# Second product of a mixture of experts: twenty products on blocks of four by three in place of seven on two by two

## The chip, the cores and the metric

The kernel runs on one core of one Trainium2 chip. The metric is device time in microseconds from launch to end, the median of several runs. All data is float32.

## The reference, cut to what matters

An attention block with sketched keys and queries gives `attn_out`; it becomes `x`, 4352 tokens of 128 values. Then comes a mixture of 8 experts, in which every token goes through every expert and is weighted by a matrix `P` that is balanced over rows and columns in turn:

```python
N, D, E, F = (4352, 128, 8, 1024)
logits = x @ w_gate
P = np.exp(logits - logits.max())
for _ in range(8):
    P /= P.sum(1, keepdims=True) + 1e-09
    P /= P.sum(0, keepdims=True) + 1e-09
    P *= N / E
for e in range(E):
    h = np.maximum(x @ w1[e], 0.0)      # first product, F = 1024 wide
    out += P[:, e:e + 1] * (h @ w2[e])  # second product
```

## The kernel before

Everything lies with features on the partitions and tokens along the free dimension. `xT` is x turned; `w1[e]` is 128 x 1024, that is 8 row blocks f of 128; `w2[e]` has 8 blocks f of 128 rows, each with two halves of 64 outputs. Every matmul of the two products has 64 output columns of weights (`tile_position=(0, H2 * s)`), so that two of them, one for the lower (s = 0) and one for the upper half (s = 1), can run beside each other on TensorE.

The unit of work is an **item**: one expert on a pair of token tiles, 2 x 480 tokens (2 x 256 for the first 512). An item has four **quads**, each of two row blocks f by two tiles. In a quad, `first(k, c)` makes the first product of one row block and one tile (L686, two matmuls into a bank `a`), and ScalarE applies the relu into `h` (L690). `combine` lets VectorE form four sums of these (L696, L698, L699, tile `t`). `seven` then lists seven products (L735) that stand for eight: a 2 x 2 by 2 x 2 block product with seven multiplications. Some of their weights are blocks of `w2`, others are sums and differences of blocks, tile `ws`, which `load_w` lets GpSimd form once per expert (L183 to L186) and then keeps in DRAM (`stored`) for the later groups. The seven products add up in four PSUM banks `s0` to `s3` (`mps`), over all row blocks and all experts of a **group**; `part` adds the four banks up into the two output tiles when a group ends, one operation at a time (`soon`, `later`), and stores them.

The groups: five plain ones with expert 0 (one for each pair of tiles) and one with expert 1, whose results are kept (`kept`) since the weights P aren't known yet, and then five weighted ones with the other experts, whose source is `xe`, x times the weight of the expert, formed by GpSimd (L531, L533) from a row of `pT` that a DMA spreads over the partitions (`pb`). Kept results are weighted by `weigh_kept` at the second expert of the group. Plain groups fill TensorE while the attention and the routing run: `fill(n)` takes n steps from the generator `steps()`, each step being one `first`, one of VectorE's sums and two of the second products, of two quads before (`LAG = 2`).

Order: the part with attention and routing has a hand-written order on VectorE and TensorE (`tc.manual_schedule`); the rest, and all of GpSimd's and SyncE's queues, are ordered by a planner. Pool `wpool` holds weights for two experts, `aps` four banks for first products, `hpool` three quads of `h` and `t`.

Of the kernel before, what the change touches and what calls it, by code (L numbers as in the profile page):

```python
# [10 lines left out]
F32 = mybir.dt.float32  # L11
# [39 lines left out]
def kernel(  # L51
# [12 lines left out]
    nc = tc.nc  # L64
# [19 lines left out]
    hpool = ctx.enter_context(tc.tile_pool(name="hpool", bufs=3))  # L84
# [4 lines left out]
    keep = ctx.enter_context(tc.tile_pool(name="keep", bufs=1))  # L89
    early = ExitStack()  # L90
# [36 lines left out]
    lgT = big.tile([P, SA, 32], F32, name="lgT")  # L127
    lgp = big.tile([P, SA, 32], F32, name="lgp")
# [15 lines left out]
    loaded = {}  # L144
# [26 lines left out]
    def load_w(e):  # L171
# [3 lines left out]
        nc.sync.dma_start(out=w2, in_=moe_w2[e].rearrange("(fo fi) d -> fi fo d", fi=P))  # L175

        ws = wpool.tile([P, 4, FO // 2, H2], F32, tag="ws", name="ws")
        if e in stored:
            nc.sync.dma_start(out=ws, in_=stored[e])
            return w1, w2, ws  # L180
# [6 lines left out]
        if e:  # L187
            stored[e] = dram.tile([P, 4, FO // 2, H2], F32, name=f"ws{e}")
            nc.sync.dma_start(out=stored[e], in_=ws)
        return w1, w2, ws  # L190

    stored = {}
# [239 lines left out]
    def routing():  # L432
# [45 lines left out]
        for b in (1, 2, 0, 3):  # L478
            nc.sync.dma_start(out=pT[:, b * S:(b + 1) * S],
                                                  in_=lgT[32 * b:32 * b + E].rearrange("p a s -> p (a s)"))  # L480
# [4 lines left out]
    sizes = [256] * 2 + [480] * 8  # L485
    starts = [sum(sizes[:i]) for i in range(len(sizes))]
    assert sum(sizes) == N
    NP = len(sizes) // 2
    PLAIN = NP
    NMAX = max(sizes)  # L490

    def pair(i):
        return starts[2 * i], sizes[2 * i]

    plain = [(i, 0) for i in range(NP)] + [(1, 1)]
    groups = [(i, [e], False) for i, e in plain]
    groups += [(i, list(range(2 if i == 1 else 1, E)), True) for i in (2, 1, *range(3, NP), 0)]
    PLAIN = len(plain)  # L500
    items = [(g, e) for g, (_, es, _) in enumerate(groups) for e in es]
    loaded_w, sources, sums, kept, parts, done = {}, {}, {}, {}, {}, {}
    soon, later = [], []

    def prepare_w(j):
        if j == 0:
            loaded_w[j] = first_w
        elif items[j - 1][1] == items[j][1]:
            loaded_w[j] = loaded_w[j - 1]
        else:  # L510
            loaded_w[j] = load_w(items[j][1])

    def weights_of(e, i):
        lo, n = pair(i)
        pb = pools[0].tile([P, 2 * NMAX], F32, tag="pb", name="pb")[:, 0:2 * n]
        nc.sync.dma_start(out=pb, in_=pT[e:e + 1, lo:lo + 2 * n].to_broadcast([P, 2 * n]))
        return pb

    def prepare_x(j):
        g, e = items[j]  # L520
        i, es, weighted = groups[g]
        lo, n = pair(i)
        if not weighted:
            sources[j] = xT[:, lo:lo + 2 * n]
            return
        pb = weights_of(e, i)
        xe = pools[0].tile([P, 2 * NMAX], F32, tag="xe", name="xe")[:, 0:2 * n]
        if j == PLAIN:
            for t in range(2):
                sl = slice(t * n, (t + 1) * n)  # L530
                nc.gpsimd.tensor_tensor(xe[:, sl], xT[:, lo:lo + 2 * n][:, sl], pb[:, sl], op=Alu.mult)  # L531
        else:
            nc.gpsimd.tensor_tensor(xe, xT[:, lo:lo + 2 * n], pb, op=Alu.mult)  # L533
        sources[j] = xe

    def weigh_kept(i):

        n = pair(i)[1]
        es = [e for p, e in plain if p == i]
        for e in es:  # L540
            pb = weights_of(e, i)
            for t in range(2):
                y = kept[i, e][t]
                nc.gpsimd.tensor_tensor(y, y, pb[:, t * n:(t + 1) * n], op=Alu.mult)  # L544
        for t in range(2):
            for e in es[1:]:
                nc.gpsimd.tensor_tensor(kept[i, es[0]][t], kept[i, es[0]][t], kept[i, e][t], op=Alu.add)

    def part(g, k):

        i, es, weighted = groups[g]
        lo, n = pair(i)
        end = g == len(groups) - 1
        lower, upper = slice(0, H2), slice(H2, P)
        s = sums[g][k]

        def tile_(tag, pool=keep, bufs=1, width=NMAX):
            return pool.tile([P, width], F32, tag=tag, name=tag, bufs=bufs)[:, 0:n]

        def at_leisure(do):  # L560

            soon.append(lambda: later.append(do))
# [4 lines left out]
        def add_now(out, a, b):  # L567
            if end:
                nc.vector.tensor_tensor(out, a, b, op=Alu.add)
            else:  # L570
                soon.append(lambda: nc.vector.tensor_tensor(out, a, b, op=Alu.add))  # L571

        def put(t):
            y = (y1, y2)[t]
            b0, nb = (lo + t * n) // 32, n // 32
            yt = pools[0].tile([P, NMAX // 32, 32], F32, tag="yt", name="yt")[:, 0:nb, :]
            nc.vector.transpose(out=yt.rearrange("p b d -> p (b d)"), in_=y)
            store(yt, b0, b0 + nb, ends[t] if end else (nc.sync,))

        own = parts.setdefault(g, {})  # L580
        if end:
            if not own:
                own.update(y=[tile_(f"y{t}", pools[0], 2) for t in range(2)], z=tile_("z"), w=tile_("w"),
                           x=tile_("m"), f=tile_("f"), r=tile_("r"))
            (y1, y2), z, w, x, f, r = (own[a] for a in "yzwxfr")
            k1, k2 = kept[i, 0]
            if k == 3:
                nc.scalar.copy(w[lower], k2[lower])
                nc.scalar.copy(r[upper], s[lower])
                add_now(w[upper], s[upper], r[upper])  # L590
                add_now(x[upper], w[upper], k1[upper])
                add_now(w[upper], w[upper], k2[upper])
            elif k == 0:
                nc.scalar.copy(z[lower], s[upper])
                nc.vector.tensor_copy(z[upper], s[lower])
                add_now(z, s, z)
                add_now(x[upper], x[upper], z[upper])
                add_now(x[lower], s[lower], k1[lower])
                add_now(z, z, w)
            elif k == 2:  # L600
                nc.scalar.copy(f[lower], s[upper])
                nc.scalar.copy(f[upper], s[upper])
                add_now(z[lower], s[lower], z[lower])
                add_now(y2, z, f)
                put(1)
            else:
                add_now(y1, s, x)
                put(0)
            return
        if not own:  # L610
            if weighted:
                own["y"] = [tile_(f"y{t}", pools[0], 2) for t in range(2)]
                own["k"] = kept[i, es[0] if (i, es[0]) in kept else 0]
            else:
                own["y"] = kept[i, es[0]] = [tile_(f"y{i}{es[0]}{t}", keep, 1, n) for t in range(2)]
        y1, y2 = own["y"]
        if k == 0:
            z = own["z"] = tile_("z")
# [4 lines left out]
        elif k == 1:  # L623
            m = own["m"] = tile_("m")
            if weighted:
                add_now(m, s, own["k"][0])
            else:
                nc.scalar.copy(m, s)
            add_now(y1[lower], own["p1"][lower], m[lower])
        elif k == 2:  # L630
            w, f = own["w"], own["f"] = tile_("w"), tile_("f")
# [3 lines left out]
            if weighted:  # L635
                add(f, f, own["k"][1])
        else:
            r = tile_("r")
# [5 lines left out]
        if all(own.get(x) for x in (0, 2, 3)) and "v" not in own:  # L644
# [4 lines left out]
            if weighted:  # L649
                at_leisure(lambda: put(1))  # L650
        if all(own.get(x) for x in range(4)):
            add(y1[upper], z[upper], m[upper])
            if weighted:
                at_leisure(lambda: put(0))
# [15 lines left out]
    quads = [(j, q) for j in range(len(items)) for q in range(FO // 2)]  # L670
    LAG = 2
    hs = {}

    def first(k, c):

        j, q = quads[k]
        n = pair(groups[items[j][0]][0])[1]
        if c == 0:
            hs[k] = (hpool.tile([P, 4, NMAX], F32, tag="h", name="h")[:, :, 0:n],
                     hpool.tile([P, 4, NMAX], F32, tag="t", name="t")[:, :, 0:n])  # L680
        f, t = 2 * q + c // 2, c % 2
        ph = bank()[:, 0:n]
        order = (0, 1) if k % 2 == 0 else (1, 0)
        for s in order:
            sl = slice(H2 * s, H2 * (s + 1))
            nc.tensor.matmul(ph[sl], loaded_w[j][0][:, P * f + H2 * s:P * f + H2 * (s + 1)],  # L686
                             sources[j][:, t * n:(t + 1) * n], start=True, stop=True,
                             tile_position=(0, H2 * s))
        h, ts = hs[k]
        nc.scalar.activation(out=h[:, c], in_=ph, func=Act.Relu)  # L690

    def combine(k):

        h, ts = hs[k]

        nc.vector.tensor_tensor(ts[:, 0:2], h[:, 1::2], h[:, 0:2], op=Alu.subtract)  # L696
        yield
# [190 lines left out]
```

## Time and profile before

| | |
|---|---|
| median of 4 runs | 957.4 us (955.93 to 957.52) |
| the profiled execution, its own time | 956.35 us |
| its span, first to last instruction | 954.5 us |
| granted clock of TensorE | 0.997 |
| TensorE busy | 939.8 us (98%) |
| VectorE busy | 562.1 us (59%) |
| ScalarE busy | 393.8 us (41%) |
| GpSimd busy | 122.4 us (13%) |
| moved by DMA | 82.34 MB, 86 GB/s over the span |

The durations below come from the one profiled execution. In its lines, PE is TensorE, PEld its weight loads, DVE VectorE, ACT ScalarE, POOL GpSimd and SP SyncE; `out<-in` are tiles by their names, `L735` is a line of the kernel. A line of the timeline has the start in us from the start of the span, the duration, the engine and the instruction; `x4` merges four records that touch. A TensorE record ends later than its successor on the same half starts, since matmuls are pipelined: what one costs is the distance of starts.

### The profile page before, as it was taken

The page shows a single profiled execution, that of the slowest core. Times are in us where ns is not written, and L with a number is a line of the kernel's source. Part 1 is how long each engine was busy: PE and PEld are TensorE (multiplying, and loading weights), DVE is VectorE, ACT ScalarE, POOL GpSimd, SP SyncE. Part 2 cuts the span into 40 slices and gives each one's busy share as a digit, 9 for nine tenths or more (in the row PEclk, how much of TensorE's full clock was granted, in tenths as well). Part 3 has the DMA queues.
Part 4 walks back from the last instruction along what each step waited for, and adds up shares of the span by engine and source line. Part 5 has one row for each costly group of instructions (what it writes and reads, how often), then busy time and mean ns, then how long its engine had stood idle before and what let it go on. Part 6 is the DMA issues. An engine that isn't in the chain of part 4 may idle for free.

```text
span 954.5 us, 13484 instructions
## 1 busy us (share of the span) xinstructions
PE 939.8 (98%) x5506; PEld 453.2 (47%) x5506; DVE 562.1 (59%) x763; ACT 393.8 (41%) x754; POOL 122.4 (13%) x105
## 2 busy tenths in 40 slices
PE   8999999999999999999999999999999999999996
PEld 6553535456666666433333333333333333346664
DVE  7787679885555546744445644444564444457555
ACT  2444345553333335333335333333443333345443
POOL 1000000142222213200001000000200000011100
PEclk9999999999999999999999999999999999999998
DMA  6600000221222232622223422222242222236430
GB/s 191 183 23 1 1 1 1 93 84 65 87 88 87 88 109 64 172 85 84 82 87 101 107 86 86 87 88 84 88 119 83 86 77 76 76 93 169 146 111 12
DMA packets 75405, 82.34 MB, mean 86 GB/s; under 512 B 22416, under 2 KB 60304, under 8 KB 75344
## 3 DMA queue, kind: packets, MB, share of 16 engines
q1 hardware_dynamic: 74320, 81.29, 27.4%
q8 instruction: 43, 0.70, 0.3%
q10 hardware_dynamic: 960, 0.13, 0.1%
q14 instruction: 18, 0.15, 0.0%
q0 software_dynamic: 64, 0.07, 0.0%
HBM read 75.44 MB, written 6.04 MB: 85 GB/s over the span
## 4 chain that ended last, share of the span: by engine, by line
PE 94%; DVE 4%; DMA 1%; issue 0%; ACT 0%; DVEq 0%; POOL 0%; POOLq 0%
PE a L686 48%; PE s L735 42%; PE a L317 1%; PE a L339 1%; PE a L286 1%; DMA ws<-ws 0%; PE a L255 0%; DVE kp L271 0%; DVE t L699 0%; DMA raw<-in_S_dram 0%; DVE qa L329 0%; DVE kT L242 0%; DVE rd L356 0%; DVE qT L237 0%; DVE t L696 0%
## 5 line engine op out<-in xcount | busy, mean ns | idle before, releaser
L686 PE MATMUL a<-xe,w 128*64 128x480 f32 (+1 forms) x2176 | 637.0, 528 | 0.0
L690 ACT ACTIVATE h<-a 128x480 f32<-128x480 f32 (+1 forms) x640 | 341.4, 534 | 515.1 <-PE a L686 509.4
L696 DVE TENSOR_TENSOR t<-h 128x960 f32<-128x960 f32 (+1 forms) x160 | 216.0, 1350 | 346.3 <-ACT h L690 346.2
L735 PE MATMUL s<-t,ws 128*64 128x480 f32 (+1 forms) x960 | 419.0, 529 | 0.0
L686 PEld LDWEIGHTS a<-xe,w 128*64 128x64 f32 x2176 | 241.8, 137 | 210.7 <-issue 160.0
L735 PE MATMUL s<-h,w 128*64 128x480 f32 (+1 forms) x640 | 286.1, 529 | 1.0 <-DVE y L571 1.0
L735 PEld LDWEIGHTS s<-t,ws 128*64 128x64 f32 x960 | 130.7, 137 | 126.5 <-issue 108.1
L735 PE MATMUL s<-t,w 128*64 128x480 f32 (+1 forms) x320 | 143.0, 529 | 0.2
L735 PE MATMUL s<-h,ws 128*64 128x480 f32 (+1 forms) x320 | 143.0, 529 | 0.0
L533 POOL TENSOR_TENSOR xe<-xT,pb 128x960 f32<-128x960 f32 (+1 forms) x33 | 67.6, 2049 | 537.5 <-PE a L686 447.1
L686 PE MATMUL a<-xT,w 128*64 128x480 f32 (+1 forms) x384 | 113.2, 540 | 1.1 <-DVE xT L358 0.9
L699 DVE TENSOR_TENSOR t<-h,t 128x480 f32<-128x480 f32 (+1 forms) x160 | 105.5, 659 | 5.4
L698 DVE TENSOR_TENSOR t<-h,t 128x480 f32<-128x480 f32 (+1 forms) x160 | 103.7, 648 | 5.1
L735 PEld LDWEIGHTS s<-h,w 128*64 128x64 f32 x640 | 87.2, 137 | 32.4 <-issue 11.1
L735 PEld LDWEIGHTS s<-t,w 128*64 128x64 f32 x320 | 43.5, 137 | 47.6 <-issue 27.2
L686 PEld LDWEIGHTS a<-xT,w 128*64 128x64 f32 x384 | 37.8, 137 | 31.8 <-issue 19.1
L735 PEld LDWEIGHTS s<-h,ws 128*64 128x64 f32 x320 | 43.7, 137 | 15.1 <-issue 5.6
L531 POOL TENSOR_TENSOR xe<-xT,pb 128x480 f32<-128x480 f32 x2 | 3.2, 1600 | 139.1 <-DVE w L571 139.1
L339 PE MATMUL a<-qa,kvz 128*64 128x352 f32 (+1 forms) x96 | 20.2, 472 | 0.3 <-DVE kvz L301 0.3
L183 POOL TENSOR_TENSOR ws<-w 128x256 f32<-128x256 f32 x8 | 6.2, 780 | 97.4 <-DMA w<-in_moe_w_dram 63.1
L544 POOL TENSOR_TENSOR y<-y,pb 128x480 f32<-128x480 f32 (+1 forms) x12 | 15.9, 1350 | 21.8 <-DMA pb<-pT 21.8
L317 PE MATMUL a<-qT,wq 64*128 64x352 f32 (+1 forms) x72 | 13.4, 490 | 1.3 <-DVE qT L237 1.3
(118 smaller groups left out, 306.0 us busy)
## 6 DMA issues: line engine op xcount, KB each, us to landing
w<-in_moe_w_dram SPq DMA_DIRECT2D x70, 512.0 KB, 4.0
ws<-ws SPq DMA_DIRECT2D x34, 512.0 KB, 3.5
pb<-pT SPq DMA_DIRECT2D x32, 480.0 KB, 3.6
kx<-in_k_dram SPq DMA_DIRECT2D x4, 544.0 KB, 3.7
qx<-in_q_dram SPq DMA_DIRECT2D x4, 544.0 KB, 5.3
v<-in_v_dram SPq DMA_DIRECT2D x32, 64.0 KB, 4.4
pb<-pT SPq DMA_DIRECT2D x8, 256.0 KB, 3.8
out_dram<-yt SPq DMA_DIRECT2D x20, 60.0 KB, 2.0
```

The source lines that it names most:

```text
L183: nc.gpsimd.tensor_tensor(ws[:, 0], a21, a22, op=Alu.add)
L286: nc.tensor.matmul(pv[64 * s:64 * (s + 1), i], kp[0:n, H * t + h].rearrange("p i j -> p (i j)"), vx[0:n, slots[h], t, :], start=(t == 0 an ...
L317: nc.tensor.matmul(banks[i][m][:, 0:n], wqf[sl, m, :], qT[sl, lo:hi], start=True, stop=True, tile_position=(64 * i, 0))
L339: nc.tensor.matmul(t[64 * i:64 * (i + 1), 0:n], kvz[:, (i + m) % 2, i].rearrange("p h d -> p (h d)"), ph[i][0][:, 0:n], start=True, stop=T ...
L533: nc.gpsimd.tensor_tensor(xe, xT[:, lo:lo + 2 * n], pb, op=Alu.mult)
L544: nc.gpsimd.tensor_tensor(y, y, pb[:, t * n:(t + 1) * n], op=Alu.mult)
L686: nc.tensor.matmul(ph[sl], loaded_w[j][0][:, P * f + H2 * s:P * f + H2 * (s + 1)], sources[j][:, t * n:(t + 1) * n], start=True, stop=True ...
L690: nc.scalar.activation(out=h[:, c], in_=ph, func=Act.Relu)
L696: nc.vector.tensor_tensor(ts[:, 0:2], h[:, 1::2], h[:, 0:2], op=Alu.subtract)
L698: nc.vector.tensor_tensor(ts[:, 2], h[:, 3], ts[:, 0], op=Alu.subtract)
L699: nc.vector.tensor_tensor(ts[:, 3], h[:, 2], ts[:, 2], op=Alu.subtract)
L735: nc.tensor.matmul(sums[g][i][H2 * s:H2 * (s + 1)], w, x, start=is_first, stop=is_last, tile_position=(0, H2 * s))
```

## The change

The weighted groups, all but the last, are cut into three tiles of 256 tokens (768) in place of two of 480, and a block of their second product is four row blocks by three tiles by two output halves, 24 plain products, done with 20. That takes other sums and other places:

- `load_w` forms or loads the old `ws` only where it is used; `sums_of_four` lets GpSimd form 16 sums of blocks of `w2` per expert in the first weighted group (six operations of 256 elements a partition, four of 128) and stores them (`stored_four`, 1 MB an expert) for the later groups. `sums_of_two` is run and stored for experts 2 to 7 in the last group of three tiles.
- `four` makes the first product of a block in eight steps, 512 tokens at once for two tiles and 256 for the third, and lets VectorE form 13 sums (and three helpers) in ten operations at the steps 2 to 9, the last two within the next block.
- `twenty` lists the products, issued at the steps 8 to 15 (`LAG = 8`, counted in steps now); they add up in sixteen places: four banks, two halves of partitions, two halves of columns.
- `part_of_twenty` ends such a group: four copies by ScalarE out of PSUM, 20 operations of 256 columns and two of 768 on VectorE, five copies across partitions by ScalarE, one at each step.
- `h` and sums lie in fixed rooms (`hb`, and `hx` once the attention's pools are closed), a quad's sums in two rooms in place of three; `xe` is multiplied in place.
- groups: plain ones (0, 2 x 256), four of 2 x 480, expert 1 on 2 x 384 and 2 x 256 tokens; weighted ones of 768 tokens from 1280, 512, 2048, 2816 and 3584 with experts 1 to 7 (2 to 7 from 512); the last, 2 x 256 tokens with experts 2 to 7, by seven products as before.

```diff
-    plain = [(i, 0) for i in range(NP)] + [(1, 1)]
-    groups += [(i, list(range(2 if i == 1 else 1, E)), True) for i in (2, 1, *range(3, NP), 0)]
+    groups = [(0, 256, 2, [0], False), *((512 + 960 * i, 480, 2, [0], False) for i in range(4)),
+              (512, 384, 2, [1], False), (0, 256, 2, [1], False)]
+    for lo in (1280, 512, 2048, 2816, 3584):
+        groups.append((lo, NT3, 3, list(range(2 if lo == 512 else 1, E)), True))
+    groups.append((0, 256, 2, list(range(2, E)), True))
...
+        for ns, x, y, off in FOURS:
+            nc.gpsimd.tensor_tensor(ws[:, c:c + len(ns)], blocks(x), blocks(y), op=Alu.subtract if off else Alu.add)
+            c += len(ns)
+        stored_four[e] = dram.tile([P, len(FORMS), FO // 4, H2], F32, name=f"ws4{e}")
+        nc.sync.dma_start(out=stored_four[e], in_=ws)
...
-        for b in (1, 2, 0, 3):
+        for b in (1, 0, 2, 3):
             nc.sync.dma_start(out=pT[:, b * S:(b + 1) * S],
...
+        order = ((0, 0), (3, 0), (3, 1), (0, 1), (1, 0), (2, 0), (1, 1), (2, 1))
+        def step(c):
+            f, last = order[c]
+            if last:
+                first(k, 4 * q + f, 2 * NT3, 3 * NT3, h[:, at(f, 2)], False)
+            else:
+                first(k, 4 * q + f, 0, 2 * NT3, h[:, f:f + 8:4], False)
...
+        def sums(c):
+            if c == 2:
+                do((U4, U2), (at(0, 0), at(3, 0)), (at(0, 1), at(3, 1)))
+            elif c == 3:
+                do((U1,), (at(3, 0),), (at(3, 2),))
+            elif c == 4:
+                do((V4,), (U1,), (at(0, 2),))
+            elif c == 6:
+                do((V3, V1), (U4, U2), (at(1, 1), at(2, 1)), True)
+                do(pqg[:, 0:2], (at(1, 1), at(3, 1)), (at(0, 1), at(2, 1)), True)
+            elif c == 7:
+                do((W1, W2), (V4, V4), pqg[:, 0:2])
+                do(pqg[:, 2], (V3,), (at(1, 0),), True)
+            elif c == 8:
+                do((U3, BB), (at(2, 0), at(1, 2)), (at(2, 2), at(2, 2)))
+            elif c == 9:
+                do((V2, W3), (U3, BB), (at(1, 2), V1))
+                nc.vector.tensor_tensor(h[:, W4], pqg[:, 2], h[:, V2], op=Alu.subtract)
...
+        return (both(0, 0, 5, 0, 2, 3), both(0, 1, 6, 2, 3, 1),
+                both(1, 0, 7, 6, 4, 5) + both(1, 0, 12, U4, 10, U2), both(1, 1, 15, V3, 13, V1),
+                both(2, 0, 1, 8, 8, 9), both(2, 0, 11, U3, 9, U1),
+                both(2, 1, 14, V2, 16, V4) + both(3, 0, 17, W1, 18, W2), both(3, 1, 20, W4, 19, W3))
...
+                if k < len(blocks) and c == 0:
+                    for i in range(2, 10):
+                        sums_at.setdefault(t + i, []).append(lambda i=i, f=sums_: f(i))
+                    if k < len(blocks) - 2:
+                        for i, ps in enumerate(products(k)):
+                            todo.setdefault(t + LAG + i, []).extend((k, p) for p in ps)
...
-                elif later and (c % 2 or share > 0.9):
+                elif later and (tiles == 3 or c % 2 or share > 0.9):
                     later.pop(0)()
```

In `both(bank, place, n, b, n2, b2)` product n goes to the lower partitions and n2 to the upper ones, b and b2 are the blocks or sums of `h` that they stream, and a product is 256 columns wide.

## The prediction

> **What bounds the kernel now.** I read the page from the top (busy shares, slices, chain), then the timeline of TensorE in three stretches, then that of VectorE where TensorE was late.
>
> ```profile
> span 954.5 us, 13484 instructions
> PE 939.8 (98%) x5506; PEld 453.2 (47%) x5506; DVE 562.1 (59%) x763; ACT 393.8 (41%) x754; POOL 122.4 (13%) x105
> PE 94%; DVE 4%; DMA 1%; issue 0%; ACT 0%; DVEq 0%; POOL 0%; POOLq 0%
> PE a L686 48%; PE s L735 42%; PE a L317 1%; PE a L339 1%; PE a L286 1%; DMA ws<-ws 0%; PE a L255 0%; DVE kp L271 0%; DVE t L699 0%; DMA raw<-in_S_dram 0%; DVE qa L329 0%; DVE kT L242 0%; DVE rd L356 0%; DVE qT L237 0%; DVE t L696 0%
> ```
>
> TensorE is busy for 98% and carries 94% of the chain, 90% in the two products. The time is the number of columns streamed, so what one product costs must be read exactly. These are first products (L686), 480 wide and then 256 wide:
>
> ```profile
> 602.94 0.97 PE L686 MATMUL a<-xe,w 128*64 128x480 f32 x4
> 604.55 0.97 PE L686 MATMUL a<-xe,w 128*64 128x480 f32 x4
> ...
> 882.27 0.60 PE L686 MATMUL a<-xe,w 128*64 128x256 f32 x4
> 883.13 0.60 PE L686 MATMUL a<-xe,w 128*64 128x256 f32 x4
> ...
> 853.84 0.57 PE L735 MATMUL s<-t,ws 128*64 128x480 f32 x1
> 854.65 0.60 PE L686 MATMUL a<-xe,w 128*64 128x256 f32 x4
> 855.08 0.57 PE L735 MATMUL s<-t,w 128*64 128x480 f32 x1
> ```
>
> Each float32 product is two records, and products for the lower and upper 64 outputs run side by side; I call a pair of concurrent records a slot. From 602.94 to 604.55 lie two slots of first and two of second product: 1.61/4 = 0.4025 us for 480 columns. From 882.27 to 883.13: 0.86/4 = 0.215 for 256. Whole items sharpen this: one expert on 2x480 tokens is 4 quads of 8 + 7 slots, 60 slots, and its first records follow each other every 24.15 us; on 2x256 tokens every 12.95. So a slot is 0.4025 or 0.2158 us: columns/1.2 ns and 2.5 ns more. The third group mixes widths: 853.84 to 855.08 is 1.24 = 2x0.4025 + 2x0.2158, so alternating widths costs nothing.
>
> **The slots, before and after.** Before: 32 items of 24.15 and 8 of 12.95 = 876.4 us. After: four plain items of 24.15 (96.6), one of 2x384 (60 slots of 384/1.2+2.5 = 322.5 ns, 19.35), eight of 12.95 (103.6; two plain, six at the end), and 34 items of 768 tokens. One of these has 8 row blocks x 2 records x (429.2 + 215.8 ns for 512 and 256 columns) = 10.32 us of first product, and 2 blocks x 20 products x 2 records / 2 side by side = 40 slots x 0.2158 = 8.63 us of second: 18.95. The old kernel gives 768 tokens 24.15 x 0.8 = 19.32. Sum after 96.6 + 19.35 + 103.6 + 644.4 = 863.95; difference **-12.45 us**. The 24 plain products of a 4x3 block (two output halves) would be 21 by sevens; 20 is under 5% less of one product only, and the 512- and 256-wide records give a little of it back in 2.5 ns each.
>
> Narrow products can suffer from weight loads. PEld loads take 137 ns each, two to a slot of 216, but the 256-wide group of before has just these and runs at 0.2158, so I charge nothing. The Trainium skill (TensorE: Matmul & The Clock Gate, Back-to-back issue gap) speaks against this: loads share the pace, so that 128 columns measured 81 ns where columns alone give 56. If those 25 ns came on each of the 34 x 56 slots of 256 columns, an estimate from that page, the change would lose 48 us and come out slower; the measured 256-wide slots say no.
>
> **VectorE.** These lines lie where a 256-wide group starts while results of a 480-wide one are still added up:
>
> ```profile
> 862.04 0.42 DVE L699 TENSOR_TENSOR t<-h,t 128x256 f32<-128x256 f32 x1
> 862.94 0.68 DVE L696 TENSOR_TENSOR t<-h 128x512 f32<-128x512 f32 x1
> 865.24 1.38 DVE L699 TENSOR_TENSOR t<-h,t 128x256 f32<-128x256 f32 x1
> 864.95 1.39 POOL L533 TENSOR_TENSOR xe<-xT,pb 128x512 f32<-128x512 f32 x1 [9.18 <-PE a L686]
> 865.95 0.59 PE L735 MATMUL s<-h,w 128*64 128x256 f32 x2
> 866.68 0.43 PE L735 MATMUL s<-t,w 128*64 128x256 f32 x1
> ```
>
> An addition of 256 columns takes 0.42 us and of 512 0.68, but 1.38 while POOL multiplies; the product that wants L699's result starts 0.3 us late (866.68, due near 866.4). This is the only wait that the steady part shows: the item from 389.4 lost 0.24 us, the one from 848.5 0.62 (16.18 against 15.56 of slots), the one from 864.7 0.36; 1.22 in all.
>
> A quad of before needs 1.16 + 2x0.66 = 2.48 us of VectorE in 6.04 us (41%). A block of after needs six additions of 512 and four of 256: 6x0.68 + 4x0.42 = 5.8 us in 9.48 (61%). Per item of 18.95 that is 11.5; the POOL multiplication delays it (L696 took 2.73 instead of 1.16 under one of 960 columns, +1.57; for 768 about +1.3): 12.9, or 68%. It stays hidden, by the distance in steps() between issue and use. A block has 8 steps of 1.18 us. The sums are issued at steps 2 to 9, the tightest are wanted five steps later (V3 and V1: 6 to 11; V2: 9 to 14), some 5.9 us, of which two operations of their own take 1.5. Without that cover each late microsecond in 68 blocks is 68 us.
>
> In the first weighted group POOL also forms 16 weight sums per expert: six of 256 columns at 0.73 us and four of 128, bounded by nothing and 0.73, taken as 0.45: 6.2 us, all 256-wide ones stretched to 1.15 if VectorE runs beside them.
>
> ```profile
> 234.25 0.73 POOL L183 TENSOR_TENSOR ws<-w 128x256 f32<-128x256 f32 x1 [11.47 <-DMA w<-in_moe_w_dram]
> 234.94 1.15 POOL L185 TENSOR_TENSOR ws<-w 128x256 f32<-128x256 f32 x1
> ```
>
> Beside these four sums (730 ns each alone) the timeline has two VectorE additions of 0.66 at 1.11 and 1.07, 0.87 more while POOL did about 1.4 us of work: some 0.6 us lost per us of it. So 12.9 + 0.6x6.2 = 16.6 of 18.95, still hidden. The Trainium skill (SBUF — State Buffer, Who interferes with whom) is harsher: an addition with two SBUF inputs and a POOL operation that reads SBUF exclude each other altogether. By it an item of this group would need 11.5 + 6.2 + 1.8 = 19.5, 0.6 over, about 4 us in 7 items. The rows agree nearly under the long multiplication (1.57 lost of 1.72 together) and not under the short sums.
>
> At the end of a three-tile group, part_of_twenty gives VectorE 20 operations of 256, an addition and a transpose of 768 (about 1.0 each): 10.4 us, one operation a step, over 27 steps or 32 us. There VectorE has 19.6 of block sums, 10.4, two multiplications (2.6) and the kept sum (about 1.5): 34 in 32. It falls 2 us behind, within the slack of some 4; 2 or 3 us more where two kept sums are weighed (tokens from 512). Bounds for five such ends: none at all, or 3 us each, 15. I take 0.5 each, nearest to the 0.24 to 0.62 of before, 2.5 in place of 1.22: **+1.3**.
>
> **The rest at nothing.** DMA per item: w1, w2 0.5 MB each, ws4 1 MB, weights 0.38 MB: 2.4 MB in 18.95 us, 127 GB/s against the page's 86 now. w2 and ws4 come free after the previous item's products (9.5 us into an item) and are wanted 18.9 us later; 512 KB landed in 3.5 us, so 1.5 MB in some 11 at worst. In the forming group SP's store of ws4 waits for POOL, and the next w1 and xe loads queue behind it by some 2 us, with 15 to spare. ScalarE: per block four activations of about 0.6 and four of 0.38, 3.9 of 9.48. The four sum banks are copied out by ScalarE at steps 1, 3, 6 and 7 and wanted six steps later. In the plain groups the sums have two rooms instead of three, so VectorE's first sum of a quad waits for the last products of two quads before, with attention work queued behind it on VectorE; those products lie one step (1.6 us) ahead of the sum and in the same step as the ScalarE result that it needs anyway, so it is late next by no more than a part of a slot. Attention and routing keep their order and have more plain work beside them (93.9 units for 88.5). The tail is the same two-tile end.
>
> Sum, against the profiled 956.35 (span 954.5 and 1.85 around it): 956.35 - 12.45 + 1.3 = 945.2. The median of the runs is 1.05 above that profile: **946.3 us**.
>
> **Rivals.** *Operands late in each block (slower).* VectorE, an in-order queue, goes from 41% to 61%, and each of its results has a due step on TensorE. If TensorE waits 0.18 us per block, 68 x 0.18 eats the gain; at 0.5 us the time is 957.4 - 12.45 + 34 = 979. For it: the late record at 866.68, and that the steady part's order isn't written by hand. Against: 4 us of slack. 0.18.
> *The forming group bound by VectorE and POOL together*: 0.6 to 1 us per item and its ends worse, 4 to 7 us: 950 to 953. For it 1.38 instead of 0.42; against, 16.6 of 18.95. 0.12.
> *The gain isn't there*: ends of groups at their upper bound, 15 - 1.2 against 12.45: 957 to 959. That is also the case if products pair badly, so that slots count 21 for 20. 0.07.
>
> **The numbers.** Forecast 0.63, with its own range 943.5 (no lost time at ends: 957.4 - 12.45 - 1.2) to 949. Faster takes forecast, forming group and a little of the third: 0.77; within 0.2% (1.9 us, about what a measurement can tell here) 0.05; slower 0.18. The range must reach into the third rival and the start of the first: 943 to 960.
>
> **What would show it.** Right: second-product records of 256 columns with slots of 0.2158, items of 768 tokens every 18.95 us, VectorE near 65 to 70% of the span, TensorE still 98%. Wrong: TensorE idle before second products and released by VectorE once per block (first rival), only in the first seven items (second), or 10 us lost where groups meet (third). Loads landing late, or slots of 256 above 0.22, would break the sum itself.

## The result and the profile after

The changed kernel takes 958.66 us (median; 957.45 to 960.65), the kernel before 956.76 beside it: ratio 1.002, 95% interval 1.0015 to 1.0025. It is slower by a fifth of a per cent; forecast were 946.3 and a gain. Its profiled span is 957.3 us against 954.5. The same lines of the page (busy shares, then the chain by engine and by line):

```profile
span 957.3 us, 18202 instructions
PE 931.0 (97%) x7162; PEld 515.0 (54%) x7162; DVE 695.4 (73%) x1195; ACT 419.0 (44%) x894; POOL 179.0 (19%) x177
PE 89%; DVE 5%; DMA 2%; POOL 1%; issue 1%; ACT 1%; DVEq 0%; SPq 0%; POOLq 0%; ACTq 0%
PE a L788 46%; PE s L931 39%; DMA pb<-pT 2%; PE a L354 1%; PE a L376 1%; POOL kept L585 1%; PE a L323 1%; DMA kx<-in_k_dram 0%; DVE hx L841 0%; DVE hb L807 0%; PE a L292 0%; DVE y L702 0%; DVE kp L308 0%; DVE qa L366 0%; DVE kT L279 0%
```

TensorE has 9 us less to do and the span is longer: there is a hole. Among the chain's entries of 1% and more two are new, the load `pb<-pT` and the multiplication `kept` (L585): both belong to `weigh_kept`, which no term of the prediction's queues held. The first products in TensorE's timeline show the end of the hole, the slow steps behind it and then the pace (second products lie between these lines):

```profile
256.07 1.98 PE L788 MATMUL a<-xe,w 128*64 128x512 f32 x4 [9.94 <-POOL xe L574]
258.69 1.92 PE L788 MATMUL a<-xe,w 128*64 128x512 f32 x4
263.30 1.02 PE L788 MATMUL a<-xe,w 128*64 128x512 f32 x4
264.59 1.02 PE L788 MATMUL a<-xe,w 128*64 128x512 f32 x4
```

TensorE waits 9.94 us for the multiplied source `xe`. Then the first two steps lie 2.62 us apart where 1.29 is the pace (263.30 to 264.59, two slots of 512 and two of 256 columns): twice as slow, since the granted clock was 0.58 from 256 to 262 (the line stands in the last section). Counted by items (the distance from one item's first record to the next one's): the one from 226.68 takes 29.39 us, the one from 256.07 21.45, and the other 31 items of 768 tokens behind it 18.95 each, to the hundredth. The hole costs 29.39 + 21.45 - 2 x 18.95 = 12.94 us: 9.94 of wait, 2.50 in the item behind it, and 0.50 because the wait is counted from the end of the last record, which lies that much behind the start that was due.

Where `xe` was is read from SyncE's queue and from GpSimd:

```profile
206.44 0.32 SPq L228 DMA_DIRECT2D ws<-ws  x1
206.81 40.49 SPq L562 DMA_DIRECT2D pb<-pT  x8
247.35 0.42 SPq L174 DMA_DIRECT2D w<-in_moe_w_dram  x1
247.83 0.42 SPq L562 DMA_DIRECT2D xe<-pT  x1
```

```profile
206.38 2.13 POOL L574 TENSOR_TENSOR xe<-xT,xe 128x768 f32<-128x768 f32 x1
212.07 1.82 POOL L585 TENSOR_TENSOR kept<-kept,pb 128x768 f32<-128x768 f32 x1 [3.56 <-DMA pb<-pT]
217.37 1.93 POOL L585 TENSOR_TENSOR kept<-kept,pb 128x768 f32<-128x768 f32 x1 [3.48 <-DMA pb<-pT]
...
252.86 1.26 POOL L587 TENSOR_TENSOR kept<-kept,kept 128x512 f32<-128x512 f32 x1
254.22 1.80 POOL L574 TENSOR_TENSOR xe<-xT,xe 128x768 f32<-128x768 f32 x1
```

Eight loads of `pb`, the weights of the kept results of *all* six weighted groups, are issued in one row as the first of these groups begins. One of them is this group's own. They share one buffer, so each waits for the multiplication of the one before: load, multiply, load, multiply, 40.49 us for the row. The next item's `w1` and `xe` stand behind them in SyncE's queue, and its multiplication (L574, 254.22) behind the eight on GpSimd. In the code the kept results are weighted at the second expert of their own group; it was the planner that put them all here, as their inputs are ready once `pT` is.

The account of the two profiled spans: -12.45 for the slots, +12.94 for the hole, +2.26 in the three items from 171.8 on (20.89, 15.21 and 18.73 us, where the slots give 20.47, 14.44 and 17.66, as part of an item's second products belong to the item before; 0.15 lost before), +1.34 in the second item of the last group (14.29 for 12.95; 1.22 lost at ends before): -12.45 + 12.94 + 2.11 + 0.12 = +2.7, and 2.8 is measured.

### The profile page after: what moved, and what is told of

It reads as the page before. It is cut to its first block, busy times and chain, and to the rows that moved or that the text cites. A ratio compares the mean times of both kernels' runs of the same rounds, so it can differ in the third digit from the quotient of the medians.

```text
span 957.3 us, 18202 instructions
## 1 busy us (share of the span) xinstructions
PE 931.0 (97%) x7162; PEld 515.0 (54%) x7162; DVE 695.4 (73%) x1195; ACT 419.0 (44%) x894; POOL 179.0 (19%) x177
## 4 chain that ended last, share of the span: by engine, by line
PE 89%; DVE 5%; DMA 2%; POOL 1%; issue 1%; ACT 1%; DVEq 0%; SPq 0%; POOLq 0%; ACTq 0%
PE a L788 46%; PE s L931 39%; DMA pb<-pT 2%; PE a L354 1%; PE a L376 1%; POOL kept L585 1%; PE a L323 1%; DMA kx<-in_k_dram 0%; DVE hx L841 0%; DVE hb L807 0%; PE a L292 0%; DVE y L702 0%; DVE kp L308 0%; DVE qa L366 0%; DVE kT L279 0%
## 5 line engine op out<-in xcount | busy, mean ns | idle before, releaser
L788 PE MATMUL a<-xe,w 128*64 128x256 f32 (+1 forms) x2560 | 518.0, 471 | 9.9 <-POOL xe L574 9.9
L792 ACT ACTIVATE hb<-a 128x256 f32<-128x256 f32 (+3 forms) x384 | 188.8, 494 | 254.5 <-PE a L788 229.8
L792 ACT ACTIVATE hx<-a 128x256 f32<-128x256 f32 (+1 forms) x368 | 170.2, 463 | 232.4 <-PE a L788 208.6
L931 PE MATMUL s<-hb,ws 128*64 128x256 f32 (+2 forms) x1312 | 235.1, 401 | 1.0 <-DVE hb L809 0.8
L841 DVE TENSOR_TENSOR hx<-hx 128x512 f32<-128x512 f32 (+1 forms) x204 | 151.9, 755 | 86.7 <-ACT hx L792 81.8
L931 PE MATMUL s<-hx,ws 128*64 128x256 f32 x1280 | 205.6, 379 | 0.2 <-DVE hx L809 0.2
L841 DVE TENSOR_TENSOR hb<-hb 128x512 f32<-128x512 f32 (+1 forms) x204 | 132.8, 661 | 95.8 <-ACT hb L792 91.5
L931 PEld LDWEIGHTS s<-hb,ws 128*64 128x64 f32 x1312 | 104.1, 138 | 119.4 <-issue 89.5
L574 POOL TENSOR_TENSOR xe<-xT,xe 128x768 f32<-128x768 f32 (+2 forms) x41 | 74.6, 1820 | 489.8 <-DMA xe<-pT 321.0
L931 PEld LDWEIGHTS s<-hx,ws 128*64 128x64 f32 x1280 | 101.9, 137 | 104.3 <-issue 73.3
L788 PE MATMUL a<-xT,w 128*64 128x480 f32 (+2 forms) x448 | 121.2, 506 | 1.3 <-DVE xT L395 1.2
```

What stands on the lines that cost most here:

```text
L574: nc.gpsimd.tensor_tensor(xe[:, sl], x[:, sl], xe[:, sl], op=Alu.mult)
L792: nc.scalar.activation(out=out, in_=ph, func=Act.Relu)
L841: nc.vector.tensor_tensor(out if not isinstance(out, tuple) else places(*out), places(*a), places(*b) if isinstance(b, tuple) else b, op=A ...
L931: nc.tensor.matmul(sums[g][i][H2 * s:H2 * (s + 1), n * place:n * (place + 1)], w, x, start=c == 1, stop=c == per, tile_position=(0, H2 * s))
```

## Experiments

The theory: the hole comes from the early issue of the kept weightings, in queues that run in order, through one buffer. The rival: VectorE and GpSimd together are too busy while weight sums are formed, and the hole is only where that shows.

**Two buffers for `pb`.**

```diff
-        pb = pools[0].tile([P, 3 * NT3], F32, tag=tag, name=tag, bufs=2 if tag == "xe" else 1)[:, 0:n]
+        pb = pools[0].tile([P, 3 * NT3], F32, tag=tag, name=tag, bufs=2)[:, 0:n]
```

> Two buffers for the kept weights' rows (pb) in place of one; nothing else. The changed kernel lost 12.9 us in the two items from 226.7 (29.39 and 21.45 us where 18.95 is the pace). Queue theory: this comes from the eight loads of pb, all issued from 206.8 on ahead of the next item's w1 and xe, each waiting for the multiplication before to free the one buffer (5 us apiece, 40 us in all). With two buffers the chain takes some 23 us, w1 and xe leave near 229 and 231, in time for 245.6: no wait, 958.7 - 12.9 = 945.7. Rival (VectorE and GpSimd too busy while weight sums are formed): the work is the same, the loss stays, 956 to 959.

Measured: 953.16 us, ratio 0.9951 (0.9935 to 0.9967), with single runs from 949.07 to 954.42. SyncE's queue, then VectorE at the same time:

```profile
207.41 23.22 SPq L562 DMA_DIRECT2D pb<-pT  x8
231.55 0.33 SPq L174 DMA_DIRECT2D w<-in_moe_w_dram  x1
```

```profile
218.74 2.29 DVE L841 TENSOR_TENSOR pqg<-hx 128x512 f32<-128x512 f32 x1
223.18 2.03 DVE L841 TENSOR_TENSOR pqg<-hx 128x256 f32<-128x256 f32 x1
228.53 2.04 DVE L619 TENSOR_TENSOR z<-z,w 128x256 f32<-128x256 f32 x1
```

The chain is 23.2 us long, as expected, and TensorE no longer waits for `xe`. But only 5.5 of the 12.9 us come back in the median, 9.6 in the fastest run; the profile is of one that took 953.79. The eight multiplications now lie between 212.93 and 236.1, with pauses of at most 2.9 us, and VectorE's additions take 2.0 to 2.3 us where 0.42 and 0.68 is their time alone; the items from 208.5 and 232.5 take 23.97 and 20.55 us, TensorE waiting for VectorE. So the queue theory names the hole, and the rival names what takes its place: by the slots they would take 17.66 and 18.95, so 7.9 us are lost, 1.1 of them as in the changed kernel. Of the 7.9, waits for VectorE's results are 5.0; the granted clock was 0.73 from 220 to 226 besides.

**One buffer, each load kept in its place.**

```diff
-        nc.sync.dma_start(out=pb, in_=pT[e:e + 1, lo:lo + n].to_broadcast([P, n]))
+        load = nc.sync.dma_start(out=pb, in_=pT[e:e + 1, lo:lo + n].to_broadcast([P, n]))
+        if tag == "pb":
+            tc.keep_in_program_order(load)
```

> One buffer pb as in the changed kernel, but each load of it is kept behind what SP was given before it, so that it is issued in its own group. Queue theory: the stall is gone, 945.7; the other kept multiplications fall into later groups, where VectorE has room, within 1 us. Rival (VectorE and GpSimd too busy): the work in the forming group falls by seven multiplications of 1.9 us, 13 us of GpSimd, and about as much is gained, so this run alone doesn't tell them apart; it does with the one before.

Measured: 949.17 us, ratio 0.992 (0.9907 to 0.9933).

```profile
228.10 0.33 SPq L174 DMA_DIRECT2D w<-in_moe_w_dram  x1
228.48 0.42 SPq L562 DMA_DIRECT2D xe<-pT  x1
228.95 0.43 SPq L562 DMA_DIRECT2D pb<-pT  x1
```

`w1` and `xe` go first and one `pb` behind them. All 33 items of 768 tokens after the first take 18.95 us; the hole is gone whole. 3.5 us are missing from 945.7. Of these, 1.9 are at the end: the last group's second and third item take 14.87 and 14.30 us instead of 12.95, 3.3 lost where the changed kernel lost 1.34, and its kept results are weighted there now. Most of the rest is no loss of this order: the item that began at 171.84 in the changed kernel begins at 172.91 here, and that start differs from run to run (below).

**The loads of `pb` from GpSimd's queue.**

```diff
-        nc.sync.dma_start(out=pb, in_=pT[e:e + 1, lo:lo + n].to_broadcast([P, n]))
+        queue = nc.gpsimd if tag == "pb" else nc.sync
+        queue.dma_start(out=pb, in_=pT[e:e + 1, lo:lo + n].to_broadcast([P, n]))
```

> One buffer pb, its loads issued from GpSimd's queue in place of SyncE's; w1 and xe no longer stand behind them on SyncE. If SyncE's queue alone held TensorE up: 945.7. If GpSimd's does as well (the eight multiplications stand ahead of the next xe multiplication, each waiting for its load): xe's load is early, its multiplication still comes after some 40 us, and the stall stays within 3 us of what it was, 956 to 960.

Measured: 964.93 us, ratio 1.0083 (1.007 to 1.0096). SyncE's queue and the longest wait of TensorE (us in all, times, longest):

```profile
227.03 0.33 SPq L174 DMA_DIRECT2D w<-in_moe_w_dram  x1
227.41 0.42 SPq L563 DMA_DIRECT2D xe<-pT  x1
```

```profile
PE a L789 <- POOL xe L575: 14.4, 1, 14.4
```

The row of `xe` is issued at 227.41, 20 us earlier than in the changed kernel, and TensorE waits longer. SyncE's queue alone is not the cause: GpSimd's own order, eight multiplications that each wait for a load, is enough. The multiplication of `xe` begins at 258.93, behind the last of them, where it began at 254.22 in the changed kernel. The size was somewhat beyond what was expected: 6.3 us more than the changed kernel where 3 was the bound.

**No weighting of kept results.** `weigh_kept` isn't called.

> Leaves out the weighting of the kept results (their loads and multiplications; they are added unweighted). Queue theory: 945.7, the same as with the order mended, which says that the kept work costs nothing where it is in order. If the kept multiplications cost through VectorE wherever they lie: 2 us or more below the run in order.

Measured: 946.93 us, ratio 0.9896 (0.9883 to 0.9909). It is 2.2 us below the run in order: the kept work isn't free there. 1.8 of it is at the last group, whose second and third item lose 1.47 us instead of 3.3.

**The kernel before, with a buffer of its own for kept weights.**

```diff
-        pb = pools[0].tile([P, 2 * NMAX], F32, tag="pb", name="pb")[:, 0:2 * n]
+        pb = pools[0].tile([P, 2 * NMAX], F32, tag="pk" if own else "pb", name="pb", bufs=1 if own else 2)[:, 0:2 * n]
```

> The kernel before, with one change: the rows that weight kept results get a buffer of their own, one in place of two shared with xe's rows. Queue theory: no twenty products are needed for the early issue; all six kept weightings should now be issued right after routing, in a chain of some 40 us from 198 on, ahead of the next w1. The old items are 24.15 us long, so w1 may come some 15 us late and still be in time for 244.7: a loss of 0 to 8 us, mostly by VectorE being slowed. If the early issue comes from the blocks of three tiles, nothing moves: 956.7.

Measured: 956.64 us, ratio 0.9996 (0.9987 to 1.0006). SyncE's queue in the kernel before, then in this run:

```profile
198.51 6.17 SPq L516 DMA_DIRECT2D pb<-pT  x2
220.50 0.33 SPq L174 DMA_DIRECT2D w<-in_moe_w_dram  x1
```

```profile
194.45 0.32 SPq L189 DMA_DIRECT2D ws<-ws  x1
194.81 31.86 SPq L516 DMA_DIRECT2D pb<-pT  x6
226.76 0.38 SPq L174 DMA_DIRECT2D w<-in_moe_w_dram  x1
```

The early row appears in the old kernel too, with nothing else changed: while kept and source rows shared two buffers, the sharing held the loads in turn. Here it costs nothing that the time shows (0.8 us in the item from 195.8), because `w1` leaves at 226.76 instead of 220.50 and isn't wanted before 244.9. So the early row alone makes no hole. The changed kernel has shorter items and also a longer row (eight loads, 40.49 us, against six, 31.86): from the start of the row to the first product that is due after it are 38.8 us there (206.81 to 245.63) and 50.1 here (194.81 to 244.91). Which of the two counts for more, no run tells.

**No weight sums for experts 1 and 2**, on top of the run in order: GpSimd writes zeros in place of the 16 sums.

> The run in order, where GpSimd only fills the 16 weight sums of experts 1 and 2 with zeros in place of forming them (leaves out these sums). The items that start at 172.9, 193.8 and 209.3 took 20.89, 15.48 and 18.73 us where the slots give 20.47, 14.44 and 17.66: 2.5 us lost while GpSimd forms both sets without a pause. If VectorE loses its time to GpSimd's sums: 949.2 - 2 = 947.2. If it is the end of attention and routing itself: 949.2.

Measured: 945.38 us, ratio 0.9883 (0.9868 to 0.9897); 3.8 us below the run in order. The items from 192.6 and 207.1 take 14.48 and 17.75 us, the slots' 14.44 and 17.66: the loss there, 2.0 us, was GpSimd's sums beside VectorE. The item before stays at 20.89. Of the rest, 0.7 is in the last group; 1.2 is the start of that item before (171.7 against 172.9), which lies between 171.5 and 173.1 in the changed kernel and its nine variants.

**Three more additions of 512 columns in each block**, on top of the run in order (`for _ in range(4)` around the first one).

> The run in order with three more additions of 512 columns in each block (the first one repeated): VectorE goes from 5.8 to 7.9 us in 9.48. If its work is hidden by the distance of issue and use, the items without weight sums stay at 18.95 (15.8 + 1.3 of 18.95), and only ends of groups and the forming group (17.1 + 3.7 = 20.8 of 18.95) lose: 8 to 20 us, 957 to 969. If VectorE were already the pace of the blocks, every item would grow by 4 us: 1085.

Measured: 974.54 us, ratio 1.0189 (1.0172 to 1.0206). The items without weight sums and away from ends of groups stay at 18.95 us, with VectorE busy for 17.18 of them in the one from 391.69: its work is hidden there, and there was room for three more additions. Three of the items in which GpSimd forms weight sums take 20.07 to 20.23, and the first of the second weighted group 19.64. The second items of the four later groups, in which kept results are weighted and the closing operations of the group before are run or just done, take 28.15, 21.90, 22.03 and 25.88: 22 us in four items, which with the forming items is more than expected.

**The last group eased**, on top of the run in order: its kept results weighted in the middle of the group before, closing operations at every third step, the addition of 768 columns as three of 256.

```diff
+                    if g == len(groups) - 2 and e == es[3]:
+                        weigh_kept(g + 1)
...
-                elif later and (tiles == 3 or c % 2 or share > 0.9):
+                elif later and (tiles == 3 or (t % 3 == 0 if g == len(groups) - 1 else c % 2) or share > 0.9):
```

> The run in order with the last group eased: its kept results are weighted in the middle of the group before, its predecessor's 27 closing operations come at every third step in place of every second, and the addition of 768 columns is three of 256. The items from 867.7 and 882.6 lost 1.92 and 1.35 us to VectorE. If GpSimd's multiplications and long operations in the short steps do it: 949.2 - 2.5 = 946.7. If VectorE's work as such is too much there: 949.2 or 1 us less.

Measured: 945.58 us, ratio 0.9885 (0.987 to 0.99): 3.6 us below the run in order; the two items take 13.20 and 12.95.

**Only the earlier weighting of it.**

> The run in order (949.2) with only the last group's kept results weighted earlier, in the middle of the group before; its closing operations as they were. The last group's second and third item lost 1.92 and 1.35 us. If GpSimd's three operations cause most: 949.2 - 2 = 947.2, since the run without kept work still lost 1.5 there. If the pace of the closing operations causes most: 948.5 or more.

Measured: 947.43 us, ratio 0.9897 (0.9883 to 0.9912): items of 14.45 and 12.95. Of the 3.3 us lost there, GpSimd's three operations cost 1.8, the pace of the closing operations and the long addition together about 1.25.

**The sums of expert 2 formed later**, on top of the eased end: a copy from the first block's relu into their tile, `nc.scalar.copy(ws[:, :, 0, 0], after)`, holds GpSimd back.

> The run with the eased end (945.6), and the weight sums of expert 2 formed later: a copy of 16 columns from the first block's relu into their tile makes GpSimd wait until the first weighted item has begun (208.7). GpSimd then no longer forms two sets without a pause beside VectorE's closing work of attention and routing. The run without these two sets got 2 us back. If it is the pile of two sets: 1 to 1.5 us gained, 944.3. If any set at that time costs as much: 945.6, with the loss moved into the item from 208.7.

Measured: 944.73 us, ratio 0.9871 (0.9855 to 0.9888), the fastest of all; the interval overlaps the one of the run with the eased end.

```profile
186.11 9.77 POOL L228 TENSOR_TENSOR ws<-w 128x256 f32<-128x256 f32 x10 [136.06 <-ACT hb L803]
195.84 4.82 POOL L584 TENSOR_TENSOR xe<-xT,xe 128x512 f32<-128x512 f32 x3
210.60 9.15 POOL L228 TENSOR_TENSOR ws<-w 128x256 f32<-128x256 f32 x10 [9.94 <-ACT ws L217]
```

The second set did move to 210.60, but the three items lose 2.25 us where they lost 2.5: the item from 208.6 gains 0.7 (18.01 for 18.73) and the one before loses 0.45. So most of the gain hoped for isn't there, and what holds the item before, from 192.7, at 15.92 for 14.44 with only one set stays open. The trace has one wait of TensorE in it, of 1.16 us to 202.50, for VectorE's closing addition `kept` of a plain group (L632).

## Why the prediction was right or wrong

**The slots: right.** 18.95 us per item of 768 tokens was predicted and is measured in 31 items, with 0.2158 us for a slot of 256 columns; alternating widths cost nothing. The 48 us that the prediction worked out from the Trainium skill (TensorE: Matmul & The Clock Gate, Back-to-back issue gap) don't appear: weight loads don't slow these 256-column records. With the order mended and the ends eased the kernel is 11 us faster than before (945.6 against 956.8), of the 12.45 that the slots give, so this term stands.

**The queues: the step that failed.** "The rest at nothing" followed the loads of an item, the store of `ws4` and the loads behind it, "some 2 us, with 15 to spare". It left out the loads and multiplications of `weigh_kept`, which had got a tag, and with it a single buffer, of their own; the kept sum was counted only for what it takes of VectorE at the ends of groups ("about 1.5"), near where the code calls it, though the front part says that SyncE's and GpSimd's order is a planner's. The term measured 12.94 us. The diff of `weights_of` had all that was needed: a buffer no longer shared with the rows that hold the order, and inputs ready at the end of routing. No rival had that mechanism. That 958.66 lies within the range of 943 to 960, and within the third rival's 957 to 959, is luck: that rival priced the ends of groups, and 1.34 us were lost there.

**VectorE in the steady part: right that it is hidden.** It has 73% of the span, somewhat above the 65 to 70 expected, hides in every block of the items away from the ends of groups, and does so with three more additions. The rival *operands late in each block* is refuted by 31 items without a wait. The forming items were sized too high, 16.6 us with what GpSimd takes: from 277.52 to 296.47 VectorE is busy for 14.26.

```profile
277.52:296.47 18.95, 18.95 (x147) 10.10 (x144) 14.26 (x21) 7.84 (x17) 10.17 (x12) 1.00 0.40 132
```

The columns after the stretch are its length, the busy time of PE, PEld, DVE, ACT and POOL, the granted clock, and DMA's share and GB/s. The loss that the second rival spoke of was not in these items but in those before them (2.26 us), where two sets of sums met the closing additions of the plain groups on VectorE (L619, L622).

**The ends of groups: too high, and wrong in place.** 2.5 us in place of 1.22 was predicted, 0.5 at each of five ends. Four of the five lost nothing, the last 1.34 in the changed kernel. It is the one with short steps.

**What went unpriced**: the pause itself costs again. The 9.94 us of wait came with another 2.5 us behind it, lost at half the pace.

## What to carry to other kernels

When a transfer gets a buffer of its own, ask what held its order until then: a planner issues what is ready, and in an in-order queue a chain through one buffer blocks everything behind it, on the queue that loads and on the engine that frees the buffer. A saving on the bounding engine shortens the time in which such a chain is hidden; check every load that is ready early against the new, shorter item. More buffers shorten the chain but may press the same work on the engine beside it; here an order kept by hand did better (949.17 us against 953.16).

## What the hardware showed

GpSimd's multiplications beside VectorE's additions: in the run with two buffers an addition of 256 columns took 2.03 us, its own 0.42 and most of one multiplication of 1.8. That agrees with the Trainium skill (SBUF — State Buffer, Who interferes with whom), where one with two SBUF inputs is shut out while GpSimd reads SBUF. Beside the short weight sums less was lost than that rule gives. In the run with three more additions an item that forms sums has 15.6 us of VectorE's own time (18 additions of 0.68, 8 of 0.42) and 8.0 of GpSimd's (six sums of 0.73, four of 0.46, one multiplication of 1.8); one after the other they would need 23.6 us, and these items took 18.95 to 20.23.

The pause of 9.94 us brought the granted clock down, to 0.58 over the 6 us after it:

```profile
256.00:262.00 6.00, 5.93 (x24) 2.52 (x26) 0.66 (x1) 1.34 (x3) 5.77 (x11) 0.58 0.00 0
```

In shorter stretches it is 1.00 from 246 to 249, 0.50 from 252 to 261 and 0.99 from 261 to 262. TensorE, back at 256.07, thus ran some 5 us at half the pace, and that is the 2.5 us lost. After 14.4 us, in the run with GpSimd's queue, it was back at 260.78 with a clock of 0.50 up to 264, and the item took 20.68, 1.7 more than the pace. A short wait was followed by the same: in the run with two buffers one of 2.26 us, up to 221.42, and then a clock of 0.50 from 223 to 226. The Trainium skill (TensorE: Matmul & The Clock Gate, What's actually happening) gives about 3.4 us at half the rate to warm up again and says that it varies between runs; the 5 us here are longer, the other two near it.
